# Turning decays, keys and queries on VectorE in 32 by 32 blocks, with unread products ahead of the early attention stages

## The chip, the core and the metric

The kernel runs on one core of a Trainium2 chip. Its time is device time in microseconds (us), as the median of several executions. TensorE is written PE, VectorE DVE, ScalarE ACT, GpSimd POOL and SyncE SP. The matrices of TensorE's path go through PSUM (its output memory), everything else lies in SBUF (on-chip memory) or DRAM.

## The reference

Three stages follow each other. Attention with a decaying state runs over 2 batches of 8 heads, 768 positions, 48 numbers a head. Its output (1536 rows of 384) goes through a dense mixture of 4 experts, and that through a mixture of 8 experts of which each row uses two.

```python
for t in range(S):                      # attention, per batch and head
    state = alpha[:, :, t, :, None] * state + einsum('bhd,bhe->bhde', k[:, :, t], v[:, :, t])
    y[:, :, t] = einsum('bhd,bhde->bhe', q[:, :, t], state)
...
for e in range(4):                      # first mixture
    out += p[:, e:e+1] * (relu(x @ w1[e]) @ w2[e])
...
for e in range(8):                      # second mixture, the two best experts of each row
    out[mask] += top2_w[mask, k, None] * (relu(x[mask] @ w1[e]) @ w2[e])
```

## The kernel before

**Units, groups and stages.** The 1536 positions are cut into seven units of 128, 256, 256, 128, 256, 256 and 256 rows. A unit's decays `a`, keys `k` and queries `q` lie as rows by heads; attention wants them turned, a head's 48 numbers across partitions. The 8 heads are taken as 4 pairs, and a group is two blocks of 128 rows by one pair: two groups in units 0 and 3, four in the others, 24 in all, named here u2g0 for unit 2, group 0. Each group runs through seven stages: `decays` (two running products, F and A, and a reciprocal), `keys`, `queries`, `keys_back`, `scores`, `states`, `outputs`.

**Turning.** `transposed` (L287) turns one block at a time on PE, as a matmul with `ident`, into the PSUM tile `tr`. It is called three times in each group, for `a`, `k` and `q`, so each call is two transposes (a pair, below). DVE then reads `tr`: scans for F and A, one multiplication for K, one for Q.

**The order.** `plan` sets a list of steps. From the third group on, groups start three steps apart, and a group's stages lie at fixed steps behind its start: decays at 0, keys at 1, queries at 2, keys_back at 3, scores at 5, states at 6, outputs at 7. `stream` writes these stages out, step by step. Each engine runs its instructions in the order written. Between the steps, `drive` writes the products of the first expert (`hidden`, `product`: L470 to L472 and L485 to L487 on PE, `hl` and `acc` on DVE), phase by phase as rows of x become ready. PE therefore stands still for as long as the next instruction in this one order waits.

**Loads.** All loads of inputs and of expert weights are issued by SP, in the order written. `load_unit` loads `a` of unit u+2 behind the decays of unit u, and `k` and `q` of unit u+1 behind the queries of unit u, in halves of two pairs; a load is one DMA for each block of 128 rows. `k` and `q` of the units from 1 on share one buffer each, `a` has two. The build gives every DMA of SP one of eight semaphores in turn, and a DMA waits until the one issued eight before it has landed.

**Start.** 12 products of a matrix of ones (L186) run on PE before the first data are there. Nothing reads them.

Of the kernel before, what the change touches and what calls it, by code (L numbers as in the profile page):

```python
# [10 lines left out]
F32 = mybir.dt.float32  # L11
# [8 lines left out]
P = 128  # L20
# [7 lines left out]
def kernel(  # L28
# [16 lines left out]
    nc = tc.nc  # L45
    B, H, S, D = q.shape
    N, DM = out.shape
    E1, _, FF = moe_w1.shape
# [3 lines left out]
    sizes = [128, 256, 256, 128, 256, 256, 256]  # L52
    phases = [(0, 128), (128, 256), (384, 384), (768, 256), (1024, 256), (1280, 256)]
    starts = [sum(sizes[:i]) for i in range(len(sizes))]
    NU = len(sizes)
    UM = max(sizes)
    BM = UM // P
    KD = DM // P
    KF = FF // P
    HP = H // 2  # L60
# [11 lines left out]
    def ps(tag, bufs=1):  # L72
        return psum.tile([P, 512], F32, tag=tag, name=tag, bufs=bufs)
# [106 lines left out]

    ones_b = const.tile([P, P], BF16, name="ones_b")
    nc.vector.memset(ones_b, 1.0)

    t = ps("g", 4)
    for _ in range(12):
        nc.tensor.matmul(t.rearrange("x (c i) -> x c i", c=4), ones_b, ones_b[:, None, :].to_broadcast([P, 4, P]),  # L186
                         start=True, stop=True)
    ident = const.tile([P, P], F32, name="ident")
    make_identity(nc, ident)
    tri = const.tile([P, P], F32, name="tri")  # L190
# [16 lines left out]
    apool = att.enter_context(tc.tile_pool(name="apool", bufs=1))  # L207
# [4 lines left out]
    for nm, n in (("a", 2), ("k", 1), ("q", 1)):  # L212
        for i in range(n):
            t = apool.tile([P, BM, H, 64], F32, name=f"x_{nm}{i}", tag=f"x_{nm}{i}")
# [7 lines left out]
    src = {"a": alpha, "q": q, "k": k, "v": v}  # L222
    V = {}

    def inputs(nm, u):
        if nm == "a":
            return X[nm, u % 2]
        return X[nm, 0] if u else early[:, "kq".index(nm)]

    def load_unit(u, names, p0=0, p1=HP):  # L230

        if u >= NU:
            return
        b, h0 = divmod(starts[u], S)
        hs = slice(2 * p0, 2 * p1)
        for nm in names:
            if nm == "v":
                V[u] = apool.tile([P, BM, H, D], F32, tag="v", name="v", bufs=2)
            for c in range(sizes[u] // P):
                frm = src[nm][b, hs, h0 + c * P:h0 + (c + 1) * P, :].rearrange("h p d -> p h d")  # L240
                if nm == "v":
                    nc.sync.dma_start(V[u][:, c, hs], frm)
                    continue
                nc.sync.dma_start(inputs(nm, u)[:, c, hs, :D], frm)
# [14 lines left out]
    for i in range(2):  # L259
        t = apool.tile([P, UM], F32, name=f"suffix{i}")  # L260
# [3 lines left out]
    for p in range(HP):  # L264
        t = apool.tile([P, BM + 1, 2 * D], F32, name=f"S{p}")
# [6 lines left out]
    def attention(u):  # L272

        b, h0 = divmod(starts[u], S)
        UB = sizes[u] // P
        first = h0 == 0
        last = h0 + sizes[u] == S
        groups = [[(g * BM // UB + i // UB, i % UB) for i in range(BM)] for g in range(HP * UB // BM)]
        st = {}
# [4 lines left out]
        def at(i):  # L284
            return slice(i * P, (i + 1) * P)

        def transposed(nm, g):  # L287
            t = ps("tr", 2)
            for i, (p, c) in enumerate(groups[g]):
                nc.tensor.transpose(t[:, at(i)], inputs(nm, u)[:, c, 2 * p:2 * p + 2, :].rearrange("x h d -> x (h d)"), ident)  # L290
            return t[:, :UM]
# [5 lines left out]
        def decays(g):  # L297
            A, K, Q, G = group("A"), group("K"), group("Q"), group("G")
            rc = apool.tile([P, BM], F32, tag="rc", name="rc", bufs=3)
            st[g] = (A, K, Q, G, rc)  # L300
            st[g, "F"] = F = next(suffixes)
            ta = transposed("a", g)
            for i in range(BM):
                o = i * P
                a = ta[:, o + 1:o + P][:, ::-1]
                nc.vector.tensor_tensor_scan(F[:, o:o + P - 1][:, ::-1], a, tri[:, 1:], 1.0, op0=OP.mult, op1=OP.bypass)
            for i in range(BM):
                nc.vector.tensor_tensor_scan(A[:, at(i)], ta[:, at(i)], tri, 1.0, op0=OP.mult, op1=OP.bypass)
            nc.vector.reciprocal(rc, A[:, P - 1::P])

        def keys(g):
            A, K, Q, G, rc = st[g]
            nc.vector.tensor_mul(K, transposed("k", g), st[g, "F"])
            for i in range(BM):
                nc.scalar.activation(G[:, at(i)], K[:, at(i)], AF.Copy, scale=rc[:, i:i + 1])

        def queries(g):
            A, K, Q, G, rc = st[g]
            nc.vector.tensor_mul(Q, transposed("q", g), A)

        def updated(g):
            return [(i, p, c) for i, (p, c) in enumerate(groups[g]) if not (last and c == UB - 1)]
# [69 lines left out]
        def loads(g, names, v):  # L392
            p0, p1 = groups[g][0][0], groups[g][-1][0] + 1
            if p1 % 2 == 0:
                load_unit(v, names, p1 - 2, p1)
# [17 lines left out]
        def queries_(g):  # L413
            queries(g)
            if u:
                loads(g, "kq", u + 1)

        def outputs_(g):
            outputs(g)
            if g == len(groups) - 1:  # L420
                load_unit(u + 2, "v")

        return len(groups), UB, (outputs_, states, keys, scores, keys_back, queries_, decays_), back

    suffixes = itertools.cycle(suffix)

    rows_at = {}
    NEAR = 2

    def plan():  # L430
        at = {}
        base = 0
        k = 0
        for u in range(NU):
            n, UB, stages, back = attention(u)
            for g in range(n):
                near = k < NEAR
                for order, (stage, off) in enumerate(zip(stages, (5, 4, 1, 3, 3, 2, 0) if near else (7, 6, 1, 5, 3, 2, 0))):
                    at.setdefault(base + off, []).append((order, k, stage, g))
                end = base + (5 if near else 7)  # L440
                base += 2 if near else 3
                k += 1
            for c in range(UB):
                at.setdefault(end + 1 + c, []).append((-1, k, back, c))
            rows_at[u] = end + 1 + UB
        return at

    steps = plan()

    def stream():  # L450
        for i in range(max(steps) + 1):
            for order, k, f, g in sorted(steps.get(i, ()), key=lambda z: z[:2]):
                f(g)
            yield

# [93 lines left out]
    for i in range(2):  # L549
        load_unit(0, "akq", i * HP // 2, (i + 1) * HP // 2)  # L550
    load_unit(0, "v")
    for what in ("a", "k", "q", 4, 0, 5, "v", 1, 6, 2, 7, 3):
        if type(what) is int:
            W.fetch(what)
        else:
            load_unit(1, what)
    W.n_raw = 2 * NG
    rows_now = stream()
    now = 0

# [523 lines left out]
```

## Time and profile before

| | |
|---|---|
| median of 3 runs | 774.01 us (773.89 to 775.78) |
| the profiled execution | 775.9 us, of which the span from the first to the last instruction is 774.2 us |
| PE busy | 757.1 us, 98% of the span |
| attention with the first expert beside it | until about 190 us |
| granted clock, 0 to 10 / 10 to 20 / 20 to 30 / behind | 1.00 / 0.58 / 0.56 / 1.00 |

Times in the views are microseconds from the start of the span. Busy time is summed over the instructions of an engine; the clock is a share of full speed.

### The profile page before, as it was taken

To read this page: it belongs to the slowest core of one execution; us is meant where nothing else is said; L and a number is where in the kernel's file an instruction comes from. 1 tells how busy PE (TensorE), PEld (TensorE's weight loads), DVE (VectorE), ACT (ScalarE), POOL (GpSimd) and SP (SyncE) were. 2 spreads that over 40 slices of the span, in tenths; PEclk is the share of its full clock that TensorE was granted. 3 is DMA by queue.
4 is the path that set the end of the run, shared out by engine and by line. 5 is a ranking of instruction groups with operands and counts; after the bars stand their busy time and mean duration, and the time that the engine had idled before them with its cause. 6 is when DMAs were issued, how large, how long until landed. Compare 5 with 4: busy or idle time off the path is not lost.

```text
span 774.2 us, 11870 instructions
## 1 busy us (share of the span) xinstructions
PE 757.1 (98%) x4630; PEld 714.8 (92%) x4630; DVE 346.7 (45%) x845; ACT 245.2 (32%) x481; POOL 161.8 (21%) x173
## 2 busy tenths in 40 slices
PE   7999999999999999999999999999999999999997
PEld 5889999999988989899899999999899999999996
DVE  5677665663222221322212335355664643754641
ACT  2533222332321022201223313323344443544430
POOL 2410000000610013100124100010343335334331
PEclk8799999999999999999999999999999999999999
DMA  9854412100530012100023200010564654654711
GB/s 169 193 114 88 87 31 41 22 1 1 173 114 0 1 41 63 60 1 1 22 61 103 92 21 11 31 31 21 182 211 123 196 172 147 190 179 145 216 60 41
DMA packets 97997, 66.96 MB, mean 86 GB/s; under 512 B 57577, under 2 KB 94500, under 8 KB 97936
## 3 DMA queue, kind: packets, MB, share of 16 engines
q1 hardware_dynamic: 89008, 51.92, 25.2%
q0 software_dynamic: 5024, 14.13, 5.7%
q10 hardware_dynamic: 3904, 0.10, 0.4%
q8 instruction: 38, 0.62, 0.3%
q14 instruction: 23, 0.19, 0.1%
HBM read 56.69 MB, written 9.82 MB: 86 GB/s over the span
## 4 chain that ended last, share of the span: by engine, by line
PE 93%; DVE 4%; ACT 1%; issue 0%; POOL 0%; POOLq 0%; DVEq 0%; ACTq 0%
PE g L470 13%; PE g L472 13%; PE g L471 13%; PE g L485 11%; PE g L487 10%; PE g L486 10%; PE g L925 3%; PE g L927 3%; PE g L926 3%; PE tr L290 2%; PE sc L382 2%; PE sc L342 2%; PE sc L356 1%; PE tr L863 1%; PE sc L378 1%; PE sc L641 1%
## 5 line engine op out<-in xcount | busy, mean ns | idle before, releaser
L476 ACT ACTIVATE hh<-g 128x384 fp32r<-128x384 f32 (+8 forms) x200 | 96.3, 485 | 281.5 <-PE g L472 273.1
L477 DVE SCALAR_TENSOR_TENSOR hl<-g,hh 128x384 fp32r<-128x384 f32 (+8 forms) x200 | 109.4, 550 | 167.5 <-ACT hh L476 157.7
L485 PE MATMUL g<-w2h,hl 128*128 128x384 f32 x464 | 162.0, 349 | 0.0
L487 PE MATMUL g<-w2h,hh 128*128 128x384 f32 x464 | 157.1, 339 | 0.0
L486 PE MATMUL g<-w2l,hh 128*128 128x384 f32 x464 | 157.1, 339 | 0.0
L470 PE MATMUL g<-xh,w1l 128*128 128x512 f32 (+2 forms) x360 | 126.6, 352 | 0.0
L471 PE MATMUL g<-xl,w1h 128*128 128x512 f32 (+2 forms) x360 | 124.1, 345 | 0.0
L472 PE MATMUL g<-xh,w1h 128*128 128x512 f32 (+2 forms) x360 | 124.0, 344 | 0.0
L485 PEld LDWEIGHTS g<-w2h,hl 128*128 128x128 f32 x464 | 87.8, 189 | 0.5
L142 POOL TENSOR_TENSOR w1l<-raw,w1h 128x768 fp32r<-128x768 f32 x16 | 29.3, 1838 | 281.7 <-ACT w1h L141 281.7
L486 PEld LDWEIGHTS g<-w2l,hh 128*128 128x128 f32 x464 | 87.9, 189 | 0.3
L487 PEld LDWEIGHTS g<-w2h,hh 128*128 128x128 f32 x464 | 87.8, 189 | 0.0
L514 DVE SCALAR_TENSOR_TENSOR acc<-g,prob,acc 128x384 f32<-128x384 f32 x36 | 22.3, 618 | 126.1 <-PE g L487 126.1
L470 PE MATMUL g<-xth,w1l 128*128 128x256 f32 (+6 forms) x216 | 73.4, 340 | 1.5 <-DVE hl L477 0.9
L471 PEld LDWEIGHTS g<-xl,w1h 128*128 128x128 f32 x360 | 67.8, 188 | 6.5 <-DVE xl L407 0.3
L472 PEld LDWEIGHTS g<-xh,w1h 128*128 128x128 f32 x360 | 67.6, 188 | 6.5
L470 PEld LDWEIGHTS g<-xh,w1l 128*128 128x128 f32 x360 | 67.7, 188 | 6.3
L471 PE MATMUL g<-xtl,w1h 128*128 128x256 f32 (+6 forms) x216 | 71.2, 330 | 0.3 <-DVE xtl L866 0.3
L472 PE MATMUL g<-xth,w1h 128*128 128x256 f32 (+6 forms) x216 | 71.2, 330 | 0.0
L141 ACT ACTIVATE w2h<-raw 128x768 fp32r<-128x768 f32 x44 | 36.5, 843 | 34.5 <-issue 23.0
L881 POOL DMA_INDIRECT out_dram<-yo,si_c x26 | 26.1, 1004 | 86.3 <-DVE yo L880 71.4
L925 PE MATMUL g<-hh,w2l 128*128 128x432 f32 (+4 forms) x120 | 43.4, 361 | 0.0
(183 smaller groups left out, 1063.6 us busy)
## 6 DMA issues: line engine op xcount, KB each, us to landing
raw<-in_moe_w_dram SPq DMA_DIRECT2D x92, 384.0 KB
v<-in_v_dram SPq DMA_DIRECT2D x12, 192.0 KB
out_dram<-zero SPq DMA_DIRECT2D x1, 2304.0 KB
x2d<-acc SPq DMA_DIRECT2D x12, 192.0 KB
x_a<-in_alpha_dram SPq DMA_DIRECT2D x20, 96.0 KB
x_k<-in_k_dram SPq DMA_DIRECT2D x18, 96.0 KB
x_q<-in_q_dram SPq DMA_DIRECT2D x18, 96.0 KB
acc<-in_moe_w_dram SPq DMA_DIRECT2D x4, 384.0 KB
```

The lines of the kernel that those rows point to most:

```text
L141: nc.scalar.activation(hi, r, AF.Copy)
L142: (nc.gpsimd if e < E1 or own else nc.vector).tensor_sub(lo, r, hi.bitcast(F32))
L470: nc.tensor.matmul(t[:, :n], wl, hx[:, kd, t0:t0 + n], start=(kd == 0), stop=False)
L471: nc.tensor.matmul(t[:, :n], wh, lx[:, kd, t0:t0 + n], start=False, stop=False)
L472: nc.tensor.matmul(t[:, :n], wh, hx[:, kd, t0:t0 + n], start=False, stop=(kd == KD - 1))
L476: nc.scalar.activation(hh[:, :n], t[:, :n], AF.Relu)
L477: nc.vector.scalar_tensor_tensor(hl[:, :n], t[:, :n], 0.0, hh.bitcast(F32)[:, :n], op0=OP.max, op1=OP.subtract)
L485: nc.tensor.matmul(t[:m, :DM], hl[:, o:o + m], wh, start=(f == 0), stop=False)
L486: nc.tensor.matmul(t[:m, :DM], hh[:, o:o + m], wl, start=False, stop=False)
L487: nc.tensor.matmul(t[:m, :DM], hh[:, o:o + m], wh, start=False, stop=(f == KF - 1))
L881: nc.gpsimd.indirect_dma_start(out=parts_of_out[s], out_offset=bass.IndirectOffsetOnAxis(ap=SLOT[e * SB + s][2][:n, e * SB + s:e * SB + s ...
L925: nc.tensor.matmul(t[:, :n], wl, hh[:, :n], start=(f == 0), stop=False)
```

## The change

From unit 2 on (`BLOCKED`), `a`, `k` and `q` are loaded so that each 32 by 32 block lies where DVE's transpose of blocks leaves it turned as attention wants it. `transposed` is then one DVE instruction for a group (128 partitions by 256), from SBUF to SBUF, in place of the two PE transposes into PSUM. A load is cut into DMAs of 32 partitions, for a pair, a head and the first 32 or last 16 of the 48 numbers; the first load into each of the four buffers comes in one piece for all pairs, behind two memsets on POOL for the numbers that are never loaded. `busy` writes unread products: 14 at the start in place of 12, two ahead of each stage in steps 0 and 1 and one ahead of each in steps 2 to 13, 49 products in all.

```diff
+    def busy(n):
+
+        t = ps("g", 4)
+        for _ in range(n):
+            nc.tensor.matmul(t.rearrange("x (c i) -> x c i", c=4), ones_b, ones_b[:, None, :].to_broadcast([P, 4, P]),
+                             start=True, stop=True)
+
+    busy(14)
...
+    BLOCKED = 2
+    padded = set()
+
+    def in_blocks(nm, u):
+
+        return inputs(nm, u).rearrange("x c h d -> x (c h d)").rearrange("x (p c y) -> x p c y", c=BM, p=HP)
+
+    def load_blocked(u, nm, p0, p1):
+        b, h0 = divmod(starts[u], S)
+        UB = sizes[u] // P
+        X_ = in_blocks(nm, u)
+        key = (nm, u % 2 if nm == "a" else 0)
+        if key not in padded:
+
+            if p1 < HP:
+                return
+            p0 = 0
+            padded.add(key)
+            every = X_.rearrange("x p c y -> x (p c y)").rearrange("x (n r) -> x n r", r=32)
+            for j in range(2):
+                nc.gpsimd.memset(every[64 * j + 32:64 * (j + 1), :, D - 32:], 1.0 if nm == "a" else 0.0)
+        for p in range(p0, p1):
+            for j in range(2):
+                for half in range(2):
+                    n = min(32, D - 32 * half)
+                    frm = src[nm][b, 2 * p + j, h0:h0 + UB * P, 32 * half:32 * half + n]
+                    to = X_[64 * j + 32 * half:64 * j + 32 * (half + 1), p, :UB].rearrange("x c y -> x (c y)")
+                    nc.sync.dma_start(to.rearrange("x (b r) -> x b r", r=32)[:, :, :n],
+                                      frm.rearrange("(b i) r -> i b r", i=32))
...
+            if u >= BLOCKED and nm != "v":
+                load_blocked(u, nm, p0, p1)
+                continue
...
-        def transposed(nm, g):
+        def transposed(nm, g, to=None):
+            if u >= BLOCKED:
+                t = to if to is not None else apool.tile([P, UM], F32, tag="T", name="T", bufs=1)
+                p, c = groups[g][0]
+                frm = in_blocks(nm, u)[:, p:p + BM // UB, c:c + UB]
+                nc.vector.transpose(t.rearrange("x (i y) -> x i y", i=BM),
+                                    frm[:, 0] if UB > 1 else frm[:, :, 0])
+                return t
...
-            nc.vector.tensor_mul(K, transposed("k", g), st[g, "F"])
+            nc.vector.tensor_mul(K, transposed("k", g, K), st[g, "F"])
...
-            nc.vector.tensor_mul(Q, transposed("q", g), A)
+            nc.vector.tensor_mul(Q, transposed("q", g, Q), A)
...
+    FIRST = 14
...
             for order, k, f, g in sorted(steps.get(i, ()), key=lambda z: z[:2]):
+                if i < FIRST:
+                    busy(2 if i < NEAR else 1)
                 f(g)
```

Three places in the written order matter below. SP, before, from the last loads of `a` for unit 3 to those of `k` and `q` for unit 2 (`DMAHW` names the semaphore of the eight, `PE` and `Pool` those of engines):

```order
L244 DMA x_a_108<-in_alpha_dram 128x4x48 [waits DMAHW1_49,PE_49]
L244 DMA x_k_110<-in_k_dram 128x4x48 [waits DMAHW2_49,PE_49]
L244 DMA x_k_110<-in_k_dram 128x4x48 [waits DMAHW3_49,PE_49]
L244 DMA x_q_112<-in_q_dram 128x4x48 [waits DMAHW4_49,PE_49]
L244 DMA x_q_112<-in_q_dram 128x4x48 [waits DMAHW5_49,PE_49]
L244 DMA x_a_108<-in_alpha_dram 128x4x48 [waits DMAHW6_49,PE_49]
L118 DMA raw<-in_moe_w_dram 128x3x256 [waits DMAHW7_49,Pool_49]
```

The same queue now, at the end of the 16 DMAs of `k` for unit 2 and the start of the 16 of `q`:

```order
L261 DMA x_k_112<-in_k_dram 32x8x16 [waits DMAHW3_49]
L261 DMA x_k_112<-in_k_dram 32x8x32 [waits DMAHW4_49]
L261 DMA x_k_112<-in_k_dram 32x8x16 [waits DMAHW5_49]
L261 DMA x_q_114<-in_q_dram 32x8x32 [waits DMAHW6_49]
L261 DMA x_q_114<-in_q_dram 32x8x16 [waits DMAHW7_49]
L261 DMA x_q_114<-in_q_dram 32x8x32 [waits DMAHW0_49]
L261 DMA x_q_114<-in_q_dram 32x8x16 [waits DMAHW1_49]
L261 DMA x_q_114<-in_q_dram 32x8x32 [waits DMAHW2_49,PE_49]
```

Where two DMAs of `k` and two of `q` stood for a half of unit 2, with no other load between them, 16 and 16 now stand for the whole. Counted in SP's order, with the first blocked DMA as the 1st, the stretch is: 16 of `a` for unit 2, two of `v`, 16 of `a` for unit 3, one of weights, 16 of `k`, then 16 of `q`; the DMAs of `q` that u2g0 reads are the 52nd to 55th, and the 9th is the first that waits for a blocked one.

DVE, before, from the K of u2g0 to its Q and the states behind it (`S` are the states, `M` the masked scores):

```order
L313 TENSOR_TENSOR K<-tr,suffix_123 128x256 [waits PE_49]
L345 TENSOR_TENSOR M<-sc_597,tri 128x256 [waits PE_49]
L345 TENSOR_TENSOR M<-sc_598,tri 128x256 [waits PE_49]
L319 TENSOR_TENSOR Q<-tr,A 128x256 [waits PE_49]
L368 SCALAR_TENSOR_TENSOR S_133<-S_133,A,sc_618 48x48 [waits PE_49]
```

The same place now:

```order
L329 STREAM_TRANSPOSE K<-x_k_112 128x256 [waits DMAHW6_49,DMAHW1_49,DMAHW7_49,DMAHW0_49,Pool_49]
L357 TENSOR_TENSOR K<-K,suffix_125 128x256 [waits DVE_49]
L389 TENSOR_TENSOR M<-sc_722,tri 128x256 [waits PE_49]
L389 TENSOR_TENSOR M<-sc_723,tri 128x256 [waits PE_49]
L329 STREAM_TRANSPOSE Q<-x_q_114 128x256 [waits DMAHW6_49,DMAHW1_49,DMAHW7_49,DMAHW0_49,Pool_49]
L363 TENSOR_TENSOR Q<-Q,A 128x256 [waits DVE_49]
L412 SCALAR_TENSOR_TENSOR S_135<-S_135,A,sc_741 48x48 [waits PE_49]
```

The waits for DMAs have moved from PE to DVE: ahead of the scores' mask M and ahead of the state update of the unit before, both in the same queue.

PE, before, at the outputs of u1g3, which read those states:

```order
L331 MATMUL tr<-ident,K 128x128 x2
L290 MATMUL tr<-ident,x_a_106 128x128 x2
...
L378 MATMUL sc_651<-S_133,Q 128x96
L382 MATMUL sc_651<-v,M 128x48 x2
L378 MATMUL sc_651<-S_133,Q 128x96
L382 MATMUL sc_651<-v,M 128x48 x2
L290 MATMUL tr<-ident,x_k_110 128x128 x2
```

The same place now:

```order
L375 MATMUL tr<-ident,K 128x128 x2
...
L422 MATMUL sc_779<-S_135,Q 128x96
L426 MATMUL sc_779<-v,M 128x48 x2
L422 MATMUL sc_779<-S_135,Q 128x96
L426 MATMUL sc_779<-v,M 128x48 x2
```

The transposes of u2g1's `a` and `k` are gone; the order of the rest is unchanged, and the second product with the states stands behind the DVE rows above.

## Rows read from the trace of the kernel before

**Rows 1.** The page, parts 1 and 4: engines, and the chain that ended last.

```profile
PE 757.1 (98%) x4630; PEld 714.8 (92%) x4630; DVE 346.7 (45%) x845; ACT 245.2 (32%) x481; POOL 161.8 (21%) x173
...
PE 93%; DVE 4%; ACT 1%; issue 0%; POOL 0%; POOLq 0%; DVEq 0%; ACTq 0%
```

**Rows 2.** Stretches: length, busy us of PE, PEld, DVE, ACT, POOL; clock; DMA; GB/s.

```profile
11.65:28.72 17.07, 16.04 (x77) 13.84 (x77) 9.14 (x30) 5.13 (x14) 1.82 (x1) 0.50 1.20 265
28.72:42.00 13.28, 12.68 (x116) 11.85 (x114) 10.72 (x39) 7.81 (x20) 7.26 (x4) 1.00 0.64 126
...
60.72:84.94 24.22, 24.12 (x200) 22.64 (x199) 18.29 (x57) 7.53 (x21) 0.54 (x1) 1.00 0.51 99
```

**Rows 3.** Timeline of PE: products on either side of four attention stages.

```profile
46.59 0.34 PE L487 MATMUL g<-w2h,hh 128*128 128x384 f32 x1
...
48.45 0.34 PE L486 MATMUL g<-w2l,hh 128*128 128x384 f32 x1
...
109.89 0.34 PE L487 MATMUL g<-w2h,hh 128*128 128x384 f32 x1
...
111.26 0.34 PE L486 MATMUL g<-w2l,hh 128*128 128x384 f32 x1
...
177.51 0.33 PE L487 MATMUL g<-w2h,hh 128*128 128x384 f32 x1
...
179.20 0.34 PE L486 MATMUL g<-w2l,hh 128*128 128x384 f32 x1
...
179.90 0.33 PE L487 MATMUL g<-w2h,hh 128*128 128x384 f32 x1
...
181.09 0.34 PE L486 MATMUL g<-w2l,hh 128*128 128x384 f32 x1
```

**Rows 4.** Timeline of SP: start, duration (sum where merged), DMA.

```profile
21.61 0.49 SPq L123 DMA_DIRECT2D acc<-in_moe_w_dram  x1
...
29.78 0.86 SPq L244 DMA_DIRECT2D x_a<-in_alpha_dram  x1
30.73 1.02 SPq L244 DMA_DIRECT2D x_k<-in_k_dram  x2
31.84 1.01 SPq L244 DMA_DIRECT2D x_q<-in_q_dram  x2
34.84 0.37 SPq L244 DMA_DIRECT2D x_a<-in_alpha_dram  x1
```

**Rows 5.** DMA traffic between 34 and 38 us, in 40 slices of 0.1 us.

```profile
GB/s 184 188 156 92 42 12 0 0 0 0 0 0 0 0 0 0 0 0 17 98 129 113 225 225 115 54 8 0 0 0 0 0 0 0 0 0 0 0 0 0
```

**Rows 6.** Timeline of PE: the unread products, u2g0 and the outputs of u1g3.

```profile
1.13 4.57 PE L186 MATMUL g<-ones_b 128*128 128x512 bf16 x12 [1.13 <-DVE ones_b L182]
...
34.54 0.38 PE L290 MATMUL tr<-ident,x_a 128*128 128x128 f32 x2
...
43.50 0.44 PE L290 MATMUL tr<-ident,x_q 128*128 128x128 f32 x2
...
47.36 0.43 PE L378 MATMUL sc<-S,Q 128*128 128x96 f32 x2
...
51.76 0.63 PE L356 MATMUL sc<-v,Kn 128*128 128x96 f32 x4
```

**Rows 7.** Timeline of DVE: one group's work, without idle time.

```profile
39.57 0.41 DVE L319 TENSOR_TENSOR Q<-tr,A 128x256 f32<-128x256 f32 x1
...
40.10 1.15 DVE L368 SCALAR_TENSOR_TENSOR S<-S,A,sc 48x48 f32<-48x48 f32 x4
41.28 0.73 DVE L306 TENSOR_TENSOR_SCAN suffix<-tr,tri 128x127 f32<-128x127 f32 x2
...
42.95 0.41 DVE L313 TENSOR_TENSOR K<-tr,suffix 128x256 f32<-128x256 f32 x1
43.40 0.76 DVE L345 TENSOR_TENSOR M<-sc,tri 128x256 f32<-128x256 f32 x2
44.08 0.41 DVE L319 TENSOR_TENSOR Q<-tr,A 128x256 f32<-128x256 f32 x1
```

More of the change, by code (lines that the diff above doesn't have):

```diff
@@ L182 @@
     nc.vector.memset(ones_b, 1.0)
[L184 to L187, printed above, removed]
+    def busy(n):
[4 more added lines that the diff above has]
+    busy(14)
     ident = const.tile([P, P], F32, name="ident")
```

## The prediction

> **What bounds the kernel now.** I read the page first: PE is busy 98% of the span, and the chain that ended last lies on PE for 93% [rows 1]. So a microsecond counts if PE no longer does it, or if PE waits for it. The table of stretches then says where PE differs. From 11.65 to 28.72 its clock was 0.50, which is 1.2 of 2.4 GHz, after the first unread products had ended at 5.7 [rows 2, 6]; DMA engines were busy all through (1.20). From 28.72 on the clock was 1.00, PE busy 12.68 of 13.28, and in the densest stretch of attention, 60.72 to 84.94, 24.12 of 24.22 with DVE at 18.29 [rows 2]. DVE is thus the next engine there, and idle a quarter of the time. Last I read SP's timeline, since the change makes many loads out of few.
>
> **What leaves PE.** 18 groups (four each in units 2, 4, 5, 6, two in unit 3) lose three pairs of transposes, 54 pairs. Matmuls overlap, so the price of a pair is not its own 0.38 to 0.44, but the distance between the same products of the expert with a pair in between and without: 48.45 − 46.59 = 1.86 against 179.20 − 177.51 = 1.69 for the key's place, 111.26 − 109.89 = 1.37 against 181.09 − 179.90 = 1.19 for the query's [rows 3]. That is 0.17 and 0.18; I take 0.18 for all three kinds, 54 x 0.18 = 9.7 us at most.
>
> **What DVE gains.** 54 transposes of 128 x 256 that the trace doesn't show. The nearest row is the multiplication of the same shape from PSUM, 0.41 [rows 7]; since both operands of the new one lie in SBUF, I take 0.40. Bounds: below, the pitch at which such instructions overlap, 44.08 + 0.41 − 43.40 − 0.76 = 0.33; above, the scans over the same 256 numbers, 0.73 [rows 7]. In the dense stretch 12 of them add 4.8 to 18.29, 23.1, while PE falls to 24.22 − 12 x 0.18 = 22.06 [rows 2]: DVE would end 1.0 later than PE there. I take +1.5 over all, for DVE in order also answers PE later. With 0.73 it is 18.29 + 8.8 − 22.06 = +5.0 in that stretch alone; with 0.33 it is 0.2.
>
> The Trainium skill says of the transposing array that it sustains one element per cycle per lane (Vector Engine (DVE) Microarchitecture Reference, section 3.8). By it 256 elements at the 0.96 GHz of the same notes would be an estimate of 0.27 plus a fixed part, near the lower bound; no row of before shows a transpose.
>
> **What SP gains, the term I trust least.** Each half of two pairs was one DMA for each 128 rows; it is eight now, and the first load into a buffer is 16 at once. SP issues one every 0.51 when nothing stops it: 1.02 for two, or 1.11 from the start of one such pair to the next [rows 4]. A single one that found the queue empty took 0.37. Landing costs 1.8: issued at 34.84, the last bytes, of the second burst, moved at about 36.65 [rows 4, 5]. SP's queue before was behind until about 30: each x_a, x_k and x_q follows within a tenth of a microsecond of the last [rows 4]. In the new order a DMA waits for the one eight before, so the 9th blocked DMA waits for the first to land, which itself waits for weights and values in the DMA engines; I take 29.0 for it. From the 9th to the 55th, the last that u2g0's queries need, are 46 issues: 46 x 0.51 = 23.5, so 52.5, landed at 54.2. Before, PE turned these queries at 43.50 [rows 6].
>
> **Who waits.** DVE's rows of the order say it: the transpose of the queries stands ahead of the states of u1g3, and PE's second product with those states (at 47.36 before [rows 6]) can't start until two of the four are updated. So: 54.2 + 0.40 (transpose) + 0.41 (Q) + 0.57 (half of the states' 1.15 [rows 7]) = 55.6 in place of 47.36, and PE idle in between, because all that stands behind in its order waits too. Then DVE is late. From one Q to the next it needs 44.08 − 39.57 = 4.51 without idle time [rows 7], and two more transposes, 5.3. Started at 54.6 it is through at 59.9, and PE's L356 behind that mask, at 51.76 before [rows 6], comes at about 60.0. PE will have stood still twice, about 40 to 47 and 50 to 55. In the stretch before 28.72 its clock stood at 0.50 [rows 2], and waits for data come with that; I add 0.7 for work at the lower clock after the waits. Lag there: 60.8 − 51.76 = **9.0**, bounds 8.3 (clock stays up) and 10.6 (3.4 us of work takes half as long again).
>
> The loads behind it (units 3 and 4) come in time for a program 9 us later: the queue has no second piece of 48 in a row.
>
> **What the unread products cost.** 49 in place of 12; the row of 12 took 4.57, so 0.38 each [rows 6]. Two more at the start hide behind the first loads. The other 35 stand in steps 0 to 13, ahead of stages in the stretch to about 55. If they hold the clock at 1.00, half of the 16.04 us of work between 11.65 and 28.72 comes back, 8.0 [rows 2], against 35 x 0.38 = 13.3 of which at most some 5 fall there; but whatever PE wins by 28.72 it loses at SP's stall, since the 55th DMA comes at its own time. Where they fall into that wait they are free. I count them as nothing: their cover is the wait for SP. Without it they would cost up to 13.3 less 8.0 = 5.3. POOL's memsets lie on an engine with 1.82 us of work in 17 [rows 2].
>
> **Sum.** Six pairs lie ahead of the 60 us point and are in its lag; 48 x 0.18 = 8.6 come off behind it. Against the profiled execution of 775.9: 775.9 + 9.0 − 8.6 + 1.5 = 777.8. That execution lies 1.9 over the median of 774.0, so for a median **775.9**.
>
> **Rivals.**
> *SP is quicker* (faster). With 0.37 a DMA [rows 4] the 46 take 17.0 instead of 23.5: 6.5 less, 769.4. With the queue free 3 us earlier, 772.9. For it: 0.37 is a row, and the new DMAs are half as large. Against: two in a row took 0.51 each whatever they carried (weights alone 0.49, keys 1.02 for two [rows 4]). It decides from a pitch of 0.42 on.
> *The queue doesn't matter at all* (faster): the stall is nothing, 774.0 − 9.7 + 1.5 = 765.8. The Trainium skill says so in general: the time to initiate a DMA is usually small relative to the DMA itself (DMA: Bandwidth & Descriptors, section Issuing engines are not separate DMA queues). Here issuing took 0.51 for a load whose bytes moved in 0.8 [rows 4, 5], and half of one will move in less than it takes to issue; so I give the rule little.
> *VectorE becomes the bound* (slower): at the scans' 0.73 the dense stretch costs 5.0 instead of 1.5 over all, the chain to 60 us 3 x 0.33 = 1.0 more: 780.4. Above 0.45 it decides. For it: it isn't known how fast DVE turns blocks. Against: a scan depends on its last element, a transpose doesn't.
> *The unread products cost more than they return* (slower): the clock stays at 0.50 and the added products delay u1g3's transposes (34.54 [rows 6]), on which the loads of unit 3's decays wait in SP's order; 13 us at full price on top of 775.9 less the 2 that fall into waits, 787.
>
> **How the numbers follow.** About 0.3% (771.7 to 776.3) is what a measurement of this kernel can tell from no change. The forecast's case, 772 to 779 by the bounds of the lag and of DVE, has 0.42: 0.30 within, 0.12 above. The quicker SP has 0.30, the queue that is no matter 0.08, VectorE 0.12, the unread products 0.08. Faster 0.38, same 0.30, slower 0.32. The range leaves out the last rival, the second, and the ends of the others: 768 to 782; that of the likeliest case alone is 772 to 779.
>
> **What the profile after would show.** SP: x_a, x_k and x_q in an unbroken row from about 29 to 53, 0.51 apart. DVE: idle ahead of L329 `Q<-x_q` between about 44 and 54, released by a DMA, and the L329 at 0.40. PE: idle ahead of the second L422 of u1g3 until about 55.6, released by DVE, and L356 of before (L400 now) near 60.8. Attention's end, at about 190 before, then comes at about 192. The forecast is wrong if DVE's wait at `Q<-x_q` is short or missing (then the gains stand alone), if L329 takes over 0.5, or if the clock's low stretch grows behind 28.72.

## The result, and the profile after

The changed kernel took 785.82 us in the median of 4 runs (785.28 to 786.46); the ratio to before is 1.0145 (95% interval 1.0129 to 1.0161). It is 11.7 us slower, outside the predicted range of 768 to 782. The profiled execution took 786.46, its span 784.7.

Parts 1 and 4 of the page of the changed kernel, engines and the chain that ended last, to be held against [rows 1]:

```profile
PE 756.2 (96%) x4559; PEld 709.2 (90%) x4559; DVE 372.9 (48%) x899; ACT 244.1 (31%) x481; POOL 165.1 (21%) x181
...
PE 83%; DVE 9%; SPq 2%; ACT 2%; DMA 2%; issue 1%; DVEq 0%; POOL 0%; POOLq 0%
```

PE has hardly less to do (the 37 added products stand against the 54 pairs), but it stands still for 28.5 us instead of 17.1 (span less busy time), and DVE, SP's queue and the DMAs have come into the chain. The table of stretches of the changed kernel (columns as in [rows 2]) says where:

```profile
11.65:28.72 17.07, 15.32 (x119) 12.34 (x119) 12.17 (x42) 7.81 (x20) 3.77 (x3) 1.00 1.15 255
28.72:42.00 13.28, 13.28 (x113) 11.76 (x113) 10.32 (x30) 6.50 (x17) 10.18 (x10) 1.00 0.40 60
42.00:52.00 10.00, 4.28 (x18) 3.95 (x17) 2.70 (x9) 1.08 (x3) 0.00 (x0) 0.72 0.47 82
52.00:60.00 8.00, 4.59 (x19) 4.33 (x19) 4.68 (x14) 0.51 (x2) 0.00 (x0) 0.50 0.42 51
60.00:73.00 13.00, 10.88 (x92) 9.86 (x90) 10.00 (x26) 5.54 (x15) 3.65 (x2) 1.00 0.51 104
73.00:85.00 12.00, 9.67 (x66) 8.71 (x65) 9.94 (x31) 2.56 (x8) 0.00 (x0) 0.82 0.39 67
```

Up to 42 the changed kernel is ahead: the clock now stands at 1.00 where it stood at 0.50. From 42 to 60 PE works for 8.9 of 18 us. From 60 to 85 it still stands idle for 4.5 of 25, and from 73 on DVE is the busier engine (9.94 against 9.67).

The first hole is the one that was predicted. SP's timeline in the changed kernel, the loads of unit 2 and unit 3's decays (sums where merged):

```profile
22.72 10.11 SPq L261 DMA_DIRECT2D x_a<-in_alpha_dram  x16
32.92 1.02 SPq L279 DMA_DIRECT2D v<-in_v_dram  x2
34.05 8.44 SPq L261 DMA_DIRECT2D x_a<-in_alpha_dram  x16
42.58 0.39 SPq L118 DMA_DIRECT2D raw<-in_moe_w_dram  x1
43.01 8.14 SPq L261 DMA_DIRECT2D x_k<-in_k_dram  x16
51.20 7.85 SPq L261 DMA_DIRECT2D x_q<-in_q_dram  x16
```

An unbroken row from 22.72 to 59.05; behind the first 16, which took 10.1, 16 took about 8.1 to 8.4: some 0.51 each. Who waits for it, on DVE and then on PE (the bracket is the idle time before the instruction and what ended it; `...` stands for rows left out):

```profile
46.88 0.45 DVE L329 STREAM_TRANSPOSE K<-x_k 128x256 f32<-128x256 f32 x1 [3.66 <-DMA x_k<-in_k_dram]
...
54.83 0.45 DVE L329 STREAM_TRANSPOSE Q<-x_q 128x256 f32<-128x256 f32 x1 [6.38 <-DMA x_q<-in_q_dram]
```

```profile
48.18 1.17 PE L400 MATMUL sc<-v,Kn 128*128 128x96 f32 x4 [5.72 <-DVE M L389]
...
56.26 0.74 PE L422 MATMUL sc<-S,Q 128*128 128x96 f32 x2 [3.41 <-DVE S L412]
...
62.60 0.69 PE L400 MATMUL sc<-v,Kn 128*128 128x96 f32 x4 [1.13 <-DVE M L389]
...
70.90 0.69 PE L400 MATMUL sc<-v,Kn 128*128 128x96 f32 x4 [0.99 <-DVE M L389]
...
79.55 0.69 PE L400 MATMUL sc<-v,Kn 128*128 128x96 f32 x4 [1.85 <-DVE M L389]
```

The queries landed at 54.8 (54.2 was predicted), the second L422 started at 56.26 (55.6). The last three rows are the second hole, which was not predicted in this size: PE waits for M in group after group, long after the loads of unit 2 are there.

The order of PE's work is the same in all kernels but for what was taken out or put in, so the same product can be compared: its start in one kernel less its start in before, here for the scores (L342 before, L386 now) that began at the time in the first line. Negative is ahead of before.

| start in before | 42.6 | 49.8 | 64.7 | 89.2 | 101.3 | 180.2 | end of the span |
|---|---|---|---|---|---|---|---|
| changed kernel | −2.6 | 10.5 | 11.1 | 15.1 | 14.6 | 10.7 | 10.5 |
| a_behind | −2.6 | 4.6 | 5.1 | 9.0 | 10.4 | 6.5 | 3.4 |
| a_behind_by_pair | −2.3 | −0.5 | 1.1 | 11.6 | 11.8 | 8.0 | 6.1 |
| twelve_unread | −0.7 | 11.3 | 11.8 | 15.7 | 15.2 | 11.4 | 7.9 |
| before_with_unread | −2.6 | −2.6 | −2.6 | −2.6 | −2.6 | −2.5 | −4.7 |
| before_idle_transposes | 0.1 | 0.8 | 0.9 | 3.3 | 3.4 | 3.7 | 4.5 |
| g_on_gpsimd | −3.3 | 11.4 | 10.2 | 11.2 | 13.8 | 7.4 | 4.6 |
| unread_ahead_of_states | −3.1 | 10.8 | 11.2 | 15.5 | 15.8 | 12.0 | 10.6 |
| blocked_from_4 | −2.1 | −2.1 | −2.2 | 4.3 | 7.8 | 4.0 | 3.5 |
| blocked_from_4_by_pair | −2.4 | −2.4 | −2.4 | 3.0 | 3.2 | −0.7 | −1.7 |
| swapped_halves | −1.9 | −1.9 | −1.9 | −2.7 | −3.2 | −7.1 | −10.0 |
| swapped_halves_g_on_gpsimd | −2.6 | −2.6 | −2.6 | −3.4 | −3.7 | −10.1 | −9.4 |
| before_unread_g_on_gpsimd | −2.6 | −2.6 | −2.6 | −2.7 | −2.7 | −2.6 | −3.2 |

For the changed kernel: 13.1 are lost between 42.6 and 49.8, another 4.0 between 65 and 89, and 4.4 come back by 180. Behind attention nothing of the change is left, and yet some profiled executions shift once more, by up to 3.3 us. Before and the changed kernel have 3.4 us at the clock 0.50 near 515 and 526, and before_with_unread and swapped_halves have none there, which gives them 1.6; the rest arises near 556 and was not followed. So what an edit does to attention is read at 180, and a difference of 2 or 3 us between whole times isn't all attention's.

### The profile page after: what moved, and what is told of

It is laid out like the page before. It is cut to its first block, busy times and chain, and to the rows that moved or that the text cites. A ratio compares the mean times of both kernels' runs of the same rounds, so it can differ in the third digit from the quotient of the medians.

```text
span 784.7 us, 12039 instructions
## 1 busy us (share of the span) xinstructions
PE 756.2 (96%) x4559; PEld 709.2 (90%) x4559; DVE 372.9 (48%) x899; ACT 244.1 (31%) x481; POOL 165.1 (21%) x181
## 4 chain that ended last, share of the span: by engine, by line
PE 83%; DVE 9%; SPq 2%; ACT 2%; DMA 2%; issue 1%; DVEq 0%; POOL 0%; POOLq 0%
PE g L518 12%; PE g L520 12%; PE g L519 12%; PE g L533 10%; PE g L535 10%; PE g L534 10%; PE g L973 3%; PE g L975 3%; PE g L974 3%; SPq L261 2%; PE sc L426 1%; PE g L187 1%; PE tr L911 1%; DVE hl L525 1%; DMA x_k<-in_k_dram 1%
```

## The experiments

Theory 1: SP's queue of blocked loads makes unit 2 wait, and that is the loss. Theory 2: DVE with the transposes can't keep up with PE, and the wait for SP only covers it. Theory 3: the unread products cost more than they return.

**a_behind** (the decays of unit u+2 loaded behind the keys and queries of unit u+1).

```diff
         def decays_(g):
             decays(g)
-            loads(g, "a", u + 2)
...
             if u:
                 loads(g, "kq", u + 1)
+            loads(g, "a", u + 2)
```

> Edit: the loads of a for unit u+2 are written behind those of k and q for unit u+1 instead of ahead of them; nothing else. Theory 1 (SP's issue queue): in the changed kernel u2g0's queries landed at 54.8, last of an unbroken row of SP's DMAs at a pitch of 0.51, and 16 DMAs of unit 3's decays (34.05 to 42.5) stood ahead of them. Without these, k is issued from about 34.5, u2g0's q from about 42.8, DVE's wait at Q<-x_q ends near 46.3 in place of 54.8, and the whole gets about 8 us shorter: 777 to 779. Theory 2 (VectorE is the bound with the transposes, and the wait for SP only covers that): most of what is taken from the wait comes back as waits for M, K and S on DVE; 782 or more. Theory 3 (the unread products cost the time): no change, 785.

779.79 us, ratio 1.0087 (1.0060 to 1.0113). The queries of u2g0 were turned at 48.82, 6.0 earlier, and the lag at 49.8 is 5.9 smaller: the wait is SP's. k could not start before 36.99, since a load of weights ahead of it now waited, so 6 came and not 8. Between 65 and 89 the lag grows by 3.9 just as it did, which is no part of theory 1.

**a_behind_by_pair** (as that, and for each pair k and q in turn).

```diff
-        for p in range(p0, p1):
-            for j in range(2):
+        for p in range(p0, p1):
+            for nm in names:
+                for j in range(2):
```

> Edit: as a_behind, and k and q of a load are issued pair by pair in turn instead of all of k and then all of q. Theory 1: u2g0 needs only the first 8 of 32 DMAs, issued by about 38.5 and landed by about 40.3, when DVE wants them at about 43; no wait for SP is left at u2g0, and the 12.5 us of lag from it go: 772 to 774. Theory 2: waits of PE for DVE's M remain all through 43 to 90 and the time stays over 778. Theory 3: 785.

781.87 us, ratio 1.0096 (1.0074 to 1.0118): over 778, as theory 2 had said, and far from theory 1's 772 to 774. The wait at u2g0 is gone (lag −0.5 at 49.8), so theory 1 holds there. But 12 are lost again by 89, at two kinds of places. Rows of PE and DVE of this kernel:

```profile
52.61 0.69 PE L401 MATMUL sc<-v,Kn 128*128 128x96 f32 x4 [2.13 <-DVE M L390]
...
69.60 0.69 PE L401 MATMUL sc<-v,Kn 128*128 128x96 f32 x4 [1.85 <-DVE M L390]
...
88.85 0.74 PE L423 MATMUL sc<-S,Q 128*128 128x96 f32 x2 [3.12 <-DVE M L390]
```

```profile
85.48 0.45 DVE L330 STREAM_TRANSPOSE K<-x_k 128x256 f32<-128x256 f32 x1 [3.24 <-DMA x_k<-in_k_dram]
```

Two are waits for M without any load missing; the third is again a load that came late. SP's row in this kernel is unbroken from 37 to past 100. Another order in a full queue moves the wait to another load.

**twelve_unread** (`busy(12)`, `FIRST = 0`).

> Edit: the unread products of before alone, 12 at the start, none ahead of the stages. Theory 1: the added 37 lie in front of the wait for SP, and what they give or take there is lost in it: 785 to 787, with the clock at 0.50 from about 12 to 28 as before, and Q<-x_q still landing near 55. Theory 3 (they cost more than they return): faster by up to 13, 773 to 780.

785.0 us, ratio 1.016 (1.013 to 1.0189), no different from the change (1.0129 to 1.0161). Its clock was 0.51 from 11.65 to 28.72 and it was 1.9 less ahead at 42.6; at 49.8 the wait for SP had evened that to 0.8. Theory 3 falls.

**before_with_unread** (the unread products in the kernel before).

> Edit: the kernel before with the unread products of the change alone (14 at the start, two ahead of each stage in steps 0 and 1, one in steps 2 to 13); no block transposes. In the changed kernel PE was 2.4 us ahead of before at 40 us, with a clock of 1.00 where it was 0.50. Theory 1: these 2.4 are kept where no wait for SP swallows them: 771.5 to 772.5. Theory 3: slower than before, 778 or more.

772.75 us, ratio 0.9972 (0.9958 to 0.9986): 2.6 ahead by 42.6 and to the end of attention, as expected. The unread products are the one part of the change that was seen to gain by itself.

**before_idle_transposes** (54 block transposes of a constant in the kernel before, read by nobody).

```diff
         def transposed(nm, g):
+            if u >= 2:
+                spare = apool.tile([P, UM], F32, tag="spare", name="spare", bufs=1)
+                nc.vector.transpose(spare.rearrange("x (i y) -> x i y", i=BM), ident[:, None, :].to_broadcast([P, BM, P]))
```

> Edit: the kernel before, and from unit 2 on DVE also turns a constant three times in each group (54 block transposes of 128 by 256 that nobody reads), ahead of the places where it reads a, k and q; PE's transposes and all loads stay as before. Theory 2, in the form that the last runs suggest: between 60 and 80 DVE's in-order row is itself a ring (K, then ScalarE's G and hh, 1.03 of waiting, hl, M, Q, S, F, A, K again) that took 6.2 a group in the kernel before, so three transposes of 0.44 come on top of each dense group: five or six groups x 1.3 less a little, 779 to 782. By the prediction's busy shares (18.29 + 12 x 0.44 = 23.6 of 24.22) nothing happens: 774 to 775.

779.74 us, ratio 1.0047 (1.0028 to 1.0065). Work of DVE alone, with no load changed, costs 3.7, most of it between 49.8 and 89; by busy shares it should have cost nothing. The ring of theory 2 (work of DVE that waits, by way of another engine, for DVE's own result) can be read off DVE's timeline of the kernel before, at two masks in the dense stretch:

```profile
65.46 0.42 DVE L477 SCALAR_TENSOR_TENSOR hl<-g,hh 128x256 fp32r<-128x256 f32 x1 [1.03 <-ACT hh L476]
65.80 0.75 DVE L345 TENSOR_TENSOR M<-sc,tri 128x256 f32<-128x256 f32 x2
...
67.26 0.42 DVE L477 SCALAR_TENSOR_TENSOR hl<-g,hh 128x256 fp32r<-128x256 f32 x1 [0.38 <-ACT hh L476]
...
71.68 0.43 DVE L477 SCALAR_TENSOR_TENSOR hl<-g,hh 128x256 fp32r<-128x256 f32 x1 [1.03 <-ACT hh L476]
72.03 0.75 DVE L345 TENSOR_TENSOR M<-sc,tri 128x256 f32<-128x256 f32 x2
```

6.23 from mask to mask, and DVE is idle twice: 0.38 ahead of one hl, where ACT itself waited for PE, and 1.03 ahead of the other. The same two masks in before_idle_transposes:

```profile
67.46 0.74 DVE L348 TENSOR_TENSOR M<-sc,tri 128x256 f32<-128x256 f32 x2
...
73.98 0.42 DVE L480 SCALAR_TENSOR_TENSOR hl<-g,hh 128x256 fp32r<-128x256 f32 x1 [1.03 <-ACT hh L479]
74.32 0.74 DVE L348 TENSOR_TENSOR M<-sc,tri 128x256 f32<-128x256 f32 x2
```

6.86 now: the 0.38 is used up, and the 1.03 is still there. What ends it shows in the changed kernel. First DVE, then ACT:

```profile
76.81 0.44 DVE L329 STREAM_TRANSPOSE K<-x_k 128x256 f32<-128x256 f32 x1
77.28 0.42 DVE L357 TENSOR_TENSOR K<-K,suffix 128x256 f32<-128x256 f32 x1
78.73 0.42 DVE L525 SCALAR_TENSOR_TENSOR hl<-g,hh 128x256 fp32r<-128x256 f32 x1 [1.03 <-ACT hh L524]
79.08 0.74 DVE L389 TENSOR_TENSOR M<-sc,tri 128x256 f32<-128x256 f32 x2
...
84.66 0.45 DVE L329 STREAM_TRANSPOSE K<-x_k 128x256 f32<-128x256 f32 x1 [0.56 <-DMA x_q<-in_q_dram]
...
86.59 0.42 DVE L525 SCALAR_TENSOR_TENSOR hl<-g,hh 128x256 fp32r<-128x256 f32 x1 [1.03 <-ACT hh L524]
86.93 0.74 DVE L389 TENSOR_TENSOR M<-sc,tri 128x256 f32<-128x256 f32 x2
```

```profile
77.74 0.69 ACT L359 ACTIVATE G<-K,rc 128x128 f32<-128x128 f32 x2 [2.66 <-DVE K L357]
78.34 0.63 ACT L524 ACTIVATE hh<-g 128x256 fp32r<-128x256 f32 x2
```

The products that the first hh reads had ended before 76, but in ACT's order G stands ahead of hh, and G waits for DVE's K. So the 1.03 that look like slack are DVE waiting for its own K, and belong to the round. In before a round of DVE that never waits for PE is thus 6.23 − 0.38 = 5.85 long. Three transposes, each 0.47 ahead of the instruction that reads it (76.81 to 77.28), make 7.26 of it. The round took 7.85 here from mask to mask (79.08 to 86.93), of which 0.56 is a wait for a load: 7.29.

**blocked_from_4** (`BLOCKED = 4`: units 2 and 3 as before).

> Edit: BLOCKED = 4 in place of 2, so units 2 and 3 are loaded and turned as before; 12 groups are left on DVE, with 36 pairs of PE's transposes gone (36 x 0.18 = 6.5). Theory 1 and 2 together: no wait at u2g0 and the dense groups keep DVE's old ring, so the unread products' gain (772.75 measured alone) and most of the 4.4 that the changed kernel won back between 97 and 195 stay: 767 to 769. Against it: unit 4's first k and q now come in one piece of 32 DMAs behind unit 3's last queries (near 90), and u4g0's q lands near 102 where it is wanted near 97; if that stops PE, 771 to 774.

778.6 us, ratio 1.0035 (1.0019 to 1.0052): the case that was named against it, and larger. DVE waited 3.27 for unit 4's first k (84.40) and 6.57 for its q (92.54).

**blocked_from_4_by_pair**.

> Edit: as blocked_from_4, and k and q of a load are issued pair by pair in turn. Theory 1: if unit 4's first q was late in blocked_from_4, it is 6 us earlier here, and the difference between the two is that wait; 767 to 768.5. If the two agree, the queue does not matter behind unit 3.

774.37 us, ratio 0.9979 (0.9967 to 0.9990). The wait for q fell to 0.45, that for k stayed (2.72 at 83.63), and with the low clock behind it (10.2 us) it cost 5.4 by 89. From 101 to 180 this kernel won 3.9.

**g_on_gpsimd** (G of the units from 2 on by POOL, so that ACT's hh does not stand behind it).

```diff
+            if u >= 2:
+                nc.gpsimd.tensor_mul(G.rearrange("x (c i) -> x c i", c=BM), K.rearrange("x (c i) -> x c i", c=BM),
+                                     rc[:, :, None].to_broadcast([P, BM, P]))
+                return
             for i in range(BM):
```

> Edit: the changed kernel with G = K x rc of the groups from unit 2 on computed by POOL in one tensor_tensor instead of by ACT in two activations, so that ACT's hh no longer stands behind G. Theory 2 as a ring over DVE and ACT: DVE's wait of 1.03 ahead of hl (K, G, hh, hl) shrinks to the 0.4 of hh, the dense groups take about 7.0 instead of 7.7, PE's waits ahead of L400 shrink, and of the 5 us of lag that arise between 65 and 89 some 3 to 4 go: 781 to 783. Theory 1 alone: 785 to 786.

781.19 us, ratio 1.0072 (1.0052 to 1.0091). The wait for SP is as long as it was, but between 65 and 89 the lag grows by 1.0 and not 4.0, and between 101 and 180 it falls by 6.4 and not 3.9. Masks stood 6.95 apart (77.14 to 84.09). This is theory 2 with its mechanism. Of the whole, less is left: from 89 to 101 this kernel lost 2.6 again, where DVE waited for the first queries of unit 4:

```profile
99.09 0.45 DVE L329 STREAM_TRANSPOSE Q<-x_q 128x256 f32<-128x256 f32 x1 [2.23 <-DMA x_q<-in_q_dram]
```

Its clock stayed at 1.00 from 62 to the end of attention, where the changed kernel had 0.50 from 80.6 to 87.4; whether it gained by that, the next run tests.

**unread_ahead_of_states** (four more unread products ahead of the states of groups 5 to 12).

```diff
+                if order == 1 and 5 <= k <= 12:
+                    busy(4)
```

> Edit: the changed kernel with four more unread products ahead of the states of groups 5 to 12, where PE waited for M (L400: 1.13 at 62.6, 0.99 at 70.9, 1.85 at 79.55). Theory: the clock's fall to 0.50 from 80.6 to 87.4 follows these waits and costs 3.4; four products of some 0.22 each fill the waits, the clock stays at 1.00 there, and the time falls by about 3: 781 to 784. If the fall does not depend on them, their cost shows: 786 to 788.

787.54 us, ratio 1.0158 (1.0133 to 1.0184). The clock did stay at 1.00 where it had fallen to 0.50 from 80.6 to 87.4, and it gave nothing back: lag 15.5 at 89, against 15.1. The same wait for M, of this kernel:

```profile
77.66 1.04 PE L187 MATMUL g<-ones_b 128*128 128x512 bf16 x4
79.67 0.69 PE L400 MATMUL sc<-v,Kn 128*128 128x96 f32 x4 [0.97 <-DVE M L389]
```

79.67, where the changed kernel had 79.55. PE was not the bound there, so its clock had no price. The next L400 came at 87.53, behind a wait for M of 1.19, where the changed kernel, at the low clock, had 87.86. My account of 3.4 us for it was wrong.

**swapped_halves** (`BLOCKED = 4`, and pairs 0 and 1 of the blocked k and q lie in the half of the buffer that unit 3 leaves free).

```diff
+    def slot(nm, p):
+        return p if nm == "a" else (p + HP // 2) % HP
...
-        key = (nm, u % 2 if nm == "a" else 0)
+        key = (nm, u % 2 if nm == "a" else p0)
...
-                    to = X_[64 * j + 32 * half:64 * j + 32 * (half + 1), p, :UB].rearrange("x c y -> x (c y)")
+                    to = X_[64 * j + 32 * half:64 * j + 32 * (half + 1), slot(nm, p), :UB].rearrange("x c y -> x (c y)")
```

> Edit: BLOCKED = 4, the queue's order as in the change, and the blocked k and q of pair p lie in place (p + 2) mod 4 of their buffers, so that pairs 0 and 1 of unit 4 go where unit 3 has no data and can be loaded a group earlier; the first load of k and q comes in two halves. Theory: blocked_from_4_by_pair was 2.4 to 2.9 ahead of before until unit 4's first k came 2.7 late, lost 5.9 there with 10.2 us at the low clock behind the wait, and won 4.4 back later. Without that wait: 774.1 - 2.4 - 4.4 = 767.3; 766 to 769. If something else than the late k stopped it at 83, 773 to 775.

767.11 us, ratio 0.9894 (0.9876 to 0.9912). No wait of DVE for a load is left in attention, and PE's longest wait from 28 to 190 is 0.7 (0.6 before).

**swapped_halves_g_on_gpsimd**.

> Edit: swapped_halves, and G of the groups from unit 4 on by POOL. Theory 2 as a ring: in g_on_gpsimd the lag fell by 6.4 between 101 and 180, all of 36 x 0.18 = 6.5, in the changed kernel by 3.9, since DVE waits there for hh behind G; so 2 less than swapped_halves: 764 to 767. If the ring does not matter in units 4 to 6: no difference.

765.97 us, ratio 0.9869 (0.9851 to 0.9887). In the profiled executions it wins 6.4 from 101 to 180 where swapped_halves wins 3.9; of the whole time 1.1 are left between the medians, and the intervals overlap a little. Its profiled execution has 3.4 us at the clock 0.50 from 503 on, which that of swapped_halves has not, and at the end of the span the two are level (764.8 and 764.2). So the gain from G is shown for attention, not for the whole. The kernel is faster than before and than the changed kernel.

**before_unread_g_on_gpsimd** (the control: G on POOL without block transposes).

> Edit: before_with_unread, and G of the groups from unit 4 on by POOL, with no block transposes. A control for swapped_halves_g_on_gpsimd: with PE's transposes in place PE never waits in units 4 to 6, so moving G alone gives nothing: 772 to 773. If it gives 2 or more, the gain there is not the ring's.

772.98 us, ratio 0.9972 (0.9960 to 0.9984), the same as before_with_unread. G's place matters only once PE's transposes are gone.

## Why the prediction was wrong

**The wait for SP: right in place and mechanism, small in size.** The pitch of 0.51, the landing at 54.2 (measured 54.8) and the second L422 at 55.6 (56.26) held. The 9th blocked DMA was issued at 28.92 (29.0), and the 55th of the count at 52.67 (52.5), so this was no luck. PE's L400 behind it, predicted at 60.8 for a lag of 9.0, came at 62.60, a lag of 10.8. The upper bound doesn't hold either: by its own words it is 8.3 + 1.7 = 10.0, not the 10.6 written. The 1.8 lie in DVE's chain, where the xl that I had left out waited 1.87 for ACT, which had G and a conversion of weights ahead of it (ACT, then DVE):

```profile
59.82 0.69 ACT L359 ACTIVATE G<-K,rc 128x128 f32<-128x128 f32 x2 [1.68 <-DVE K L357]
60.42 0.83 ACT L141 ACTIVATE w1h<-raw 128x768 fp32r<-128x768 f32 x1
61.16 0.84 ACT L450 ACTIVATE xh<-tr 128x384 fp32r<-128x384 f32 x2
```

```profile
61.65 0.56 DVE L451 TENSOR_TENSOR xl<-tr,xh 128x384 fp32r<-128x384 f32 x1 [1.87 <-ACT xh L450]
```

Moving the loads moved the wait (a_behind), and taking them off unit 2 took it away (blocked_from_4, lag −2.1 at 49.8).

**DVE's +1.5: the step that failed.** From that L400 on, the prediction had −8.6 from PE's pairs and +1.5 from DVE, −7.1; the changed kernel went from 10.8 to 10.5, −0.3. The price of a transpose was near (0.44 measured, 0.40 taken, so +0.5 a stretch of 12). What was wrong is the comparison "23.1 against 22.06" of busy times, which read DVE as idle a quarter of the time. DVE's busy time leaves out the 1.03 that it waits for hh behind G, behind its own K. Counted with it, the round shown of before had 0.38 of slack, not a quarter, and three transposes take 1.4. In the changed kernel the round came to 7.29, where PE was to have 22.06 / 4 = 5.5 a group. before_idle_transposes prices the transposes alone at 3.7 by the end of attention; g_on_gpsimd takes 3.0 off the 4.0 that the changed kernel loses between 65 and 89. The rival "VectorE becomes the bound" had this outcome; but its condition, above 0.45 a transpose, came from busy times too, and 0.44 was enough.

By the rate in the Trainium skill (Vector Engine (DVE) Microarchitecture Reference, section 3.8) the estimate for a transpose was 0.27 and a fixed part; the rows show 0.44, so 0.17 beside it. The Trainium skill's sentence that the time to initiate a DMA is usually small relative to the DMA (DMA: Bandwidth & Descriptors, section Issuing engines are not separate DMA queues) doesn't hold here: at some 0.51 each the issuing set the start of unit 2.

**The sum of the miss.** 785.8 − 775.9 = 9.9: 1.8 in the lag, 6.8 behind it, where DVE had +1.5, and 1.3 because the profiled execution of before stood 1.9 over its median and that of the changed kernel 0.6. Not all of the 6.8 is the round: some 0.8 of it are the waits for loads at 84 and 92, and about 1.0 is a multiplication that DVE ran beside POOL (last section), for both of which the prediction had nothing. This division is read from rows and was not tested.

**What held.** A pair is worth what was read: with G out of the way, the 36 pairs of units 4 to 6 gave 7.5 from 82 on (10.1 − 2.6), 0.21 each, where 0.18 was taken. The unread products hold the clock, gain 2.6 where nothing swallows it (before_with_unread) and nothing in the change (twelve_unread): they were counted as nothing. The clock's low stretch did grow behind 28.72, which was named as a sign of being wrong (0.50 from 46.4 to 60.1 and from 80.6 to 87.4); the second of these cost nothing (unread_ahead_of_states), the first was not priced. The loads of units 3 and 4 came in time, by no more than luck of the lag: DVE waited 0.56 and 0.20 for them at 84 and 92; in g_on_gpsimd, a_behind_by_pair and blocked_from_4 such loads were the next wait. I had called the queue free behind unit 2; it is full to the end of attention's loads, near 162.

**Open.** How the changed kernel would do with all units blocked and a queue that keeps up wasn't tried; the loads would have to be fewer or issued elsewhere. Nor was the change's collision with POOL taken out by itself.

## What to carry to other kernels

A busy share of 75% is no slack if the engine's idle time ends in something that waits for the engine itself. Follow each regular wait (here 1.03) back through the other engines, and if it returns to the same engine, add it to the round, and compare rounds, not busy times. When a change makes one transfer into eight, count issues per group against the time of a group for the whole run: in a full queue another order only moved the wait to another load. And look for the part of a change that gains where nothing else stands in its way: here units 4 to 6 alone, with a free half of a buffer for the first load, 1.1% faster instead of 1.5% slower.

## What the runs showed of the hardware

Vector instructions with two inputs in SBUF took about three times as long while POOL ran a tensor_tensor on SBUF; a transpose, with one input, kept its time. In the changed kernel, DVE and POOL:

```profile
39.70 2.37 DVE L350 TENSOR_TENSOR_SCAN suffix<-T,tri 128x127 f32<-128x127 f32 x2
...
71.10 0.43 DVE L329 STREAM_TRANSPOSE Q<-x_q 128x256 f32<-128x256 f32 x1
71.56 1.42 DVE L363 TENSOR_TENSOR Q<-Q,A 128x256 f32<-128x256 f32 x1
```

```profile
39.98 1.81 POOL L142 TENSOR_TENSOR w1l<-raw,w1h 128x768 fp32r<-128x768 f32 x1 [1.10 <-issue]
...
70.87 1.84 POOL L142 TENSOR_TENSOR w1l<-raw,w1h 128x768 fp32r<-128x768 f32 x1 [7.73 <-ACT w1h L141]
```

2.37 for two scans that took 0.73 elsewhere [rows 7], 1.42 for a multiplication of 0.43: POOL's instructions end at 41.79 and 72.71, DVE's some 0.28 behind each. Before, these scans and multiplications read one of their operands from PSUM, and kept their times beside POOL (0.41 for the K at 42.95 [rows 7]). The Trainium skill (SBUF — State Buffer, section Who interferes with whom) says that a vector instruction with two inputs in SBUF contends with a GpSimd instruction that reads SBUF, and one with at most one such input does not; it calls the shared port pair an exclusive lock. These places agree. So block transposes into SBUF also turn readers of PSUM into instructions that POOL can hold up. In the first case DVE waited for k anyway; the second made one round of the dense stretch about 1.0 longer. No run tested it by itself.

In the changed kernel the clock was 0.50 from 80.6 to 87.4, behind PE's wait of 1.85 that ended at 79.55. In unread_ahead_of_states, where unread products left 0.97 of that wait, it stayed at 1.00, as it did in before_with_unread through all of attention.
